# The last queries' scores as two products over equal halves of the keys

## The chip, the cores and the metric

The kernel runs on one core of one Trainium2 chip. The metric is the device time of one execution in microseconds (us); of several runs the median is given. Matrix products run on TensorE (PE in the profile, its weight loads PEld), most elementwise work on VectorE (DVE), exponentials and casts on ScalarE (ACT), some scaling and subtracting on GpSimd (POOL), and nearly all transfers are issued from one queue, that of SyncE (SP).

## The reference

Block-causal attention feeds two feed-forward layers, all in float32:

```python
scores = scale * np.matmul(q, k.transpose(0, 1, 3, 2))   # q, k, v: (4, 8, 576, 64)
mask = block_i >= block_j                                # blocks of 64 positions
scores = np.where(mask, scores, -1000000000.0)
scores = scores - np.max(scores, axis=-1, keepdims=True)
attn = np.exp(scores)
attn = attn / (np.sum(attn, axis=-1, keepdims=True) + 1e-09)
attn_out = np.matmul(attn, v)
...
h = x @ w_in;  x = (h * sigmoid(h)) @ w_out              # 2304 tokens, 512 -> 2048 -> 512
h = x @ w_in2; x = (np.maximum(h, 0) + alpha * np.minimum(h, 0)) @ w_out2
```

The last block of 64 queries of each head (positions 512 to 575) sees all 576 keys, so it needs no mask.

## The kernel before

Float32 accuracy is had from three products each: every operand is split into a high and a low part, and high*high, high*low and low*high are summed in PSUM. `product` (L546) yields the three matmuls of a score tile, `three` (L794) those of the feed-forward layers; all feed-forward matmuls carry L797.

Attention is cut into jobs, one for a batch and a pair of heads. Eight `FirstJob`s and eight `Job`s of kind 0 do the first 256 queries; sixteen `Job`s of kind 1 do queries 256 to 511 and the last 64. A job of kind 1 has, in the order of its steps, `scores(2)` (six matmuls with 384 keys, the two heads in the two halves of the array's rows), `scores(3)` (the same with 512 keys), `last_scores` (the change), and their `weights`, which divide by the sum, split in two float16 parts on POOL (L648) and DVE (L650), and turn the tile by a DMA; `output` (L671, products with the values) and `last_output` (L741) come a job or two later. `bound` is one small product (L528), `prepare` casts queries and keys for a later job on ACT (three activations that write `qk`) and DVE (L515, L518).

`last_scores` handles the last 64 queries of both heads at once: 128 query rows by 576 keys. 576 float32 columns are more than one PSUM bank of 512, so the scores take two tiles, `s` and `s2`: 512 keys and 64 keys. The row maximum is the smaller of two negated maxima (L692, L694, L696), then two activations take the exponential with that bias and sum it (`p` from `s`, `pb` from `s2`). All score tiles come in turn from a ring of PSUM tags `"ees"` (two buffers of `e`, one of `s`): `scores(2)` takes an `e` and the `s`, `scores(3)` two of `e`, `last_scores` the `s` and an `e`. So the `scores(2)` of the next job can write `s` only when the exponential has read the `s` of this job's `last_scores`.

The feed-forward work of layer 1 runs between: `up1` (tile `h`, 24 matmuls of 256 columns for a pair of weight tiles) and `down1` (tile `acc`, 24 likewise) alternate, in chunks of 256 tokens; two such pairs go with one job. When a chunk is done `store1` scales its two accumulators into tiles `x2e` (ACT, DVE) and a DMA writes them out; `x2e` shares the two buffers of tag `t` with the tanh tiles of `act1`. Layer 2 follows when attention is over.

The order of all instructions on all engines is made ahead by a list scheduler, `Plan.order` (L131): every step has an engine, a cost (`pe_cost`, `dve_cost`, `act_cost`, ...), what it reads and writes, and a due time `at`; the engine that can start first takes, of the steps that are ready, the one with the smallest due time. A change in a cost can so move steps on every engine:

```python
start = max(free, min(o.ready for o in lst))
...
o = min((o for o in ready[e] if o.ready <= start), key=lambda o: (o.at, o.index))
```

## Time and profile before

| | us |
|---|---|
| median of 3 runs | 988.57 (987.9 to 990.77) |
| the profiled execution | 991.2 |
| its span, first to last instruction | 989.4 |
| PE busy | 965.6 (98% of the span) |
| PEld busy | 889.6 (90%) |
| DVE busy | 634.5 (64%) |
| ACT busy | 392.5 (40%) |
| POOL busy | 255.4 (26%) |

The profile shows one execution. The busy time of PE counts matmuls whose ends are modelled and overlap, so what a matmul costs in a row of them is read from the starts: the start of the next one less its own. The sixteen jobs of kind 1 with their feed-forward work lie between about 211 and 467 us from the start of the span, layer 2 after about 585 us.

### The profile page before, as it was taken

The numbers are of one execution on the slowest core, as the hardware profiler recorded it, in microseconds if no ns is written. First come the engines' busy times: TensorE is split into PE (matmuls) and PEld (weight loads), VectorE is DVE, ScalarE is ACT, GpSimd is POOL, SyncE is SP. The second block draws the span as 40 slices with busy tenths as digits, with TensorE's granted clock in tenths as the row PEclk, the third lists the DMA queues.
The fourth block names the chain that finished last, engine by engine and source line by source line (L and its number), as shares of the span: only waits on it lengthen the run. The fifth ranks groups of instructions, "written<-read, shape, count | busy, mean of one in ns | idle before, by whom it ended". The sixth has DMA issues, their size and how long they took to land.

```text
span 989.4 us, 18146 instructions
## 1 busy us (share of the span) xinstructions
PE 965.6 (98%) x7072; PEld 889.6 (90%) x7072; DVE 634.5 (64%) x1365; ACT 392.5 (40%) x904; POOL 255.4 (26%) x312
## 2 busy tenths in 40 slices
PE   7889999999999999999999999999999999999998
PEld 5789999899999989999999989999999999999997
DVE  5999976668877778787124999844444444444443
ACT  5876744445555555554224555421111211211111
POOL 2632222435444445454223550010100100100000
PEclk9989999999999999999999999999999999999999
DMA  9940333456685765654215970010010100000100
GB/s 367 360 169 23 76 97 102 73 111 129 108 164 111 145 128 132 122 120 89 37 54 204 331 253 1 1 64 1 1 64 1 64 1 1 33 1 1 32 1 32
DMA packets 124469, 94.04 MB, mean 95 GB/s; under 512 B 98400, under 2 KB 109792, under 8 KB 124384
## 3 DMA queue, kind: packets, MB, share of 16 engines
q1 hardware_dynamic: 124384, 92.90, 35.2%
q8 instruction: 55, 0.90, 0.4%
q14 instruction: 30, 0.25, 0.1%
HBM read 60.37 MB, written 9.96 MB: 71 GB/s over the span
## 4 chain that ended last, share of the span: by engine, by line
PE 83%; DVE 10%; DMA 3%; issue 2%; ACT 2%; POOL 0%; SPq 0%; POOLq 0%; DVEq 0%; ACTq 0%
PE h L797 27%; PE acc L797 24%; PE e L797 15%; PE s L797 7%; PE e L550 3%; PE s L550 2%; PE o L671 2%; DMA pT<-p 1%; DMA x<-x2e 1%; DVE ws1i L344 1%; PE o L741 1%; DVE p L650 1%; DVE t L830 1%; PE o L528 1%; DVE g L311 1%
## 5 line engine op out<-in xcount | busy, mean ns | idle before, releaser
L797 PE MATMUL h<-xh,w0i 128*128 128x256 f32 x1728 | 231.9, 288 | 3.4 <-DVE w0i L311 3.2
L797 PEld LDWEIGHTS h<-xh,w0i 128*128 128x128 f32 x1728 | 217.8, 194 | 6.7 <-DVE w0i L311 3.4
L797 PE MATMUL acc<-g,w0o 128*128 128x256 f32 x1536 | 203.3, 286 | 3.8 <-DVE g L311 3.7
L797 PEld LDWEIGHTS acc<-g,w0o 128*128 128x128 f32 x1536 | 190.0, 191 | 6.4 <-DVE g L311 5.4
L301 ACT ACTIVATE g<-u 128x384 fp32r<-128x384 f32 x96 | 50.2, 523 | 267.5 <-DVE u L915 265.9
L797 PE MATMUL e<-w1o,g 128*128 128x512 f32 x576 | 148.8, 394 | 0.0
L797 PEld LDWEIGHTS e<-w1o,g 128*128 128x128 f32 x576 | 106.7, 188 | 16.8
L797 PE MATMUL acc<-xh,w1i 128*128 128x384 f32 x576 | 109.1, 337 | 0.0
L797 PE MATMUL h<-xh,w1i 128*128 128x384 f32 x576 | 108.9, 337 | 0.0
L797 PEld LDWEIGHTS acc<-xh,w1i 128*128 128x128 f32 x576 | 102.4, 188 | 4.2
L797 PEld LDWEIGHTS h<-xh,w1i 128*128 128x128 f32 x576 | 102.3, 188 | 4.0
L830 DVE SCALAR_TENSOR_TENSOR t<-t,h 128x512 f32<-128x512 f32 x72 | 49.0, 681 | 62.5 <-ACT t L301 62.1
L311 DVE TENSOR_TENSOR g<-u,g 128x384 fp32r<-128x384 f32 x96 | 54.4, 567 | 53.8 <-ACT g L301 53.8
L648 POOL TENSOR_SCALAR p<-p,stat 128x384 f16<-128x384 f32 (+3 forms) x96 | 60.3, 635 | 105.0 <-ACT g L301 35.1
L311 POOL TENSOR_TENSOR xh<-xs,xh 128x384 fp32r<-128x384 f32 x20 | 21.0, 1082 | 244.9 <-ACT xh L301 244.9
L311 POOL TENSOR_TENSOR g<-t,g 128x512 fp32r<-128x512 f32 x48 | 66.4, 1384 | 67.7 <-ACT g L301 64.2
L797 PE MATMUL s<-w1o,g 128*128 128x512 f32 x288 | 82.0, 392 | 0.0
L301 ACT ACTIVATE t<-h 128x512 f32<-128x512 f32 x72 | 42.8, 595 | 90.4 <-PE h L797 79.9
L650 DVE SCALAR_TENSOR_TENSOR p<-p,stat,p 128x384 f16<-128x384 f32 (+3 forms) x96 | 68.8, 732 | 11.6 <-POOL p L648 11.5
L913 DVE TENSOR_SCALAR u<-acc,alpha_sb 128x384 f32<-128x384 f32 x48 | 29.6, 617 | 72.0 <-PE acc L797 71.8
L913 DVE TENSOR_SCALAR u<-h,alpha_sb 128x384 f32<-128x384 f32 x48 | 29.6, 616 | 68.6 <-PE h L797 68.6
L797 PEld LDWEIGHTS s<-w1o,g 128*128 128x128 f32 x288 | 54.1, 188 | 12.5
(121 smaller groups left out, 1244.5 us busy)
## 6 DMA issues: line engine op xcount, KB each, us to landing
st<-qkv_b SPq DMA_DIRECT2D x16, 800.0 KB, 5.1
raw0i<-w_in SPq DMA_DIRECT2D x16, 512.0 KB, 10.2
raw0o<-w_out SPq DMA_DIRECT2D x16, 512.0 KB, 10.3
raw1i<-w_in SPq DMA_DIRECT2D x16, 512.0 KB, 5.2
raw1o<-w_out SPq DMA_DIRECT2D x16, 512.0 KB, 4.8
x<-x2e SPq DMA_DIRECT2D x18, 256.0 KB, 4.1
st<-qkv_first SPq DMA_DIRECT2D x8, 512.0 KB, 7.3
st<-qkv_a SPq DMA_DIRECT2D x8, 512.0 KB, 3.6
```

The source lines that it names most:

```text
L301: nc.scalar.activation(dst(), src(), func, **k)
L311: eng.tensor_tensor(lo(), src(), hi().bitcast(F32), op=ALU.subtract)
L344: add("DVE", dve_cost(512), lambda: nc.vector.scalar_tensor_tensor(t(), t(), 3, low(), op0=ALU.logical_shift_left, op1=ALU.bitwise_or), [t ...
L528: add("PE", 0.25, lambda: nc.tensor.matmul(t()[:, 0:128], am()[:, 0:1].to_broadcast([128, 128]), eye_sb(), start=True, stop=True), [am, ey ...
L550: yield lambda n=n, a=a, b=b: nc.tensor.matmul(dst, w[rows, a, q0:q0 + m], w[rows, b, nq + k0:nq + k1], start=(n == 0), stop=(n == 2))
L648: add("POOL", pool_cost(n), lambda hl=hl, rr=rr, pr=pr: nc.gpsimd.tensor_scalar(hl()[:, :, 0], pr(), rr(), 1.0, op0=ALU.mult, op1=ALU.mult ...
L650: add("DVE", dve_cost(n, 1, 1), lambda hl=hl, rr=rr, pr=pr: nc.vector.scalar_tensor_tensor(hl()[:, :, 1], pr(), rr(), hl()[:, :, 0], op0=A ...
L671: nc.tensor.matmul(o()[64 * r:64 * r + 64, q0:T1], self.v(r, kt, cv), self.pT[r][1]()[:, 2 * kt + cp, q0:T1], start=(kt == 0 and n == 0), ...
L741: nc.tensor.matmul(o()[64 * r:64 * r + 64, 0:64], self.v(r, kt, cv), pT()[:, run, 64 * r:64 * r + 64], start=(run == 0 and cv == 0), stop= ...
L797: nc.tensor.matmul(dst, lhs(a), rhs(b), start=(start and n == 0), stop=(stop and n == 2))
L830: add("DVE", dve_cost(2 * T1), lambda: nc.vector.scalar_tensor_tensor(t(), t(), 1.0, h3(), op0=ALU.add, op1=ALU.mult), [t, h], [t])
L913: add("DVE", dve_cost(T2, 1, 1), lambda: nc.vector.tensor_scalar(u(), h()[:, 0:T2], 0.0, alpha_sb()[:, m:m + 1], op0=ALU.min, op1=ALU.mult ...
```

## The change

The 576 keys are cut into 288 and 288 in place of 512 and 64. The cost that the scheduler is given for the products goes from three matmuls of 512 columns and three counted as 100 to six of 288. There are still two maxima, now over 288 columns each. `p` (512 columns) and `pb` (64) keep their shapes, so the exponential takes three activations: 288 columns from `s` and 224 from `s2` into `p`, 64 from `s2` into `pb`, with three sums. The two small DVE steps of `last_weights` before the reciprocal add three sums in place of two and then the 1e-9; their number stays three.

```diff
@@ -684,33 +684,34 @@
             x = sb(att_p, [128, 10], F32, "stat", 4, name="stat4")
             s, s2 = ps_scores(self.k), ps_scores(self.k)
             def products():
-                for dst, a, b in ((s, 0, 512), (s2, 512, 576)):
+                for dst, a, b in ((s, 0, 288), (s2, 288, 576)):
                     for f in self.product(dst()[:, 0:b - a], slice(0, 128), 256, 128, a, b):
                         f()
 
-            add("PE", pe_cost(*[512] * 3, *[100] * 3), products, [qk], [s, s2], after=self.beside(-1, "output"))
-            add("DVE", dve_cost(512), lambda: nc.vector.tensor_reduce(
-                x()[:, 0:1], s(), axis=AX.X, op=ALU.max, negate=True), [s], [(x, 0)])
-            add("DVE", dve_cost(64), lambda: nc.vector.tensor_reduce(
-                x()[:, 1:2], s2()[:, 0:64], axis=AX.X, op=ALU.max, negate=True), [s2], [(x, 0)])
+            add("PE", pe_cost(*[288] * 6), products, [qk], [s, s2], after=self.beside(-1, "output"))
+            for n, half in enumerate((s, s2)):
+                add("DVE", dve_cost(288), lambda n=n, half=half: nc.vector.tensor_reduce(
+                    x()[:, n:n + 1], half()[:, 0:288], axis=AX.X, op=ALU.max, negate=True), [half], [(x, 0)])
             add("DVE", dve_cost(80), lambda: nc.vector.tensor_tensor(
                 x()[:, 2:3], x()[:, 0:1], x()[:, 1:2], op=ALU.min), [(x, 0)], [(x, 1)])
             p = sb(att_p, [128, 512], F32, "p", 3)
             pb = sb(att_p, [128, 64], F32, "p4b", 2)
             bias = lambda: x()[:, 2:3]
-            act(512, lambda: p(), lambda: s(), AF.Exp, [s, (x, 1)], [p, (x, 2)], psum=True,
-                bias=bias, accum_out=lambda: x()[:, 4:5])
-            act(64, lambda: pb(), lambda: s2()[:, 0:64], AF.Exp, [s2, (x, 1)], [pb, (x, 3)], psum=True,
-                bias=bias, accum_out=lambda: x()[:, 5:6])
+            for n, (dst, src, a, b) in enumerate((
+                (lambda: p()[:, 0:288], s, 0, 288), (lambda: p()[:, 288:512], s2, 0, 224), (lambda: pb(), s2, 224, 288),
+            )):
+                act(b - a, dst, lambda src=src, a=a, b=b: src()[:, a:b], AF.Exp, [src, (x, 1)],
+                    [(p, n) if n < 2 else pb, (x, 2 + n)], psum=True, bias=bias, accum_out=lambda n=n: x()[:, 4 + n:5 + n])
             self.xp[4] = x, p, pb
 
         def last_weights(self):
             x, p, pb = self.xp.pop(4)
-            add("DVE", dve_cost(1, 1, 1), lambda: nc.vector.tensor_scalar(
-                x()[:, 6:7], x()[:, 4:5], x()[:, 5:6], EPS, op0=ALU.add, op1=ALU.add), [(x, 2), (x, 3)], [(x, 4)])
+            add("DVE", dve_cost(1, 1, 2), lambda: nc.vector.tensor_scalar(
+                x()[:, 7:8], x()[:, 4:5], x()[:, 5:6], x()[:, 6:7], op0=ALU.add, op1=ALU.add),
+                [(x, 2), (x, 3), (x, 4)], [(x, 5)])
             add("DVE", dve_cost(1), lambda: nc.vector.tensor_scalar(
-                x()[:, 6:7], x()[:, 6:7], 2.0**-P_EXP, None, op0=ALU.mult), [(x, 4)], [(x, 4)])
-            add("DVE", dve_cost(6), lambda: nc.vector.reciprocal(x()[:, 8:9], x()[:, 6:7]), [(x, 4)], [(x, 5)])
+                x()[:, 7:8], x()[:, 7:8], EPS, 2.0**-P_EXP, op0=ALU.add, op1=ALU.mult), [(x, 5)], [(x, 5)])
+            add("DVE", dve_cost(6), lambda: nc.vector.reciprocal(x()[:, 8:9], x()[:, 7:8]), [(x, 5)], [(x, 6)])
             rr = lambda: x()[:, 8:9]
             p16 = self.parts16(0)
             hl = lambda: p16()[:, 0:8].rearrange("p (j c) m -> p j c m", c=2)
@@ -721,10 +722,10 @@
             ):
                 b = pb if key else p
                 add("POOL", pool_cost(n), lambda src=src, hi=hi: nc.gpsimd.tensor_scalar(
-                    hi(), src(), rr(), 1.0, op0=ALU.mult, op1=ALU.mult), [b, (x, 5)], [(p16, key)])
+                    hi(), src(), rr(), 1.0, op0=ALU.mult, op1=ALU.mult), [b, (x, 6)], [(p16, key)])
                 add("DVE", dve_cost(n, 1, 1), lambda src=src, hi=hi, lo=lo: nc.vector.scalar_tensor_tensor(
                     lo(), src(), rr(), hi(), op0=ALU.mult, op1=ALU.subtract),
-                    [b, (x, 5), (p16, key)], [(p16, key + 1)])
+                    [b, (x, 6), (p16, key)], [(p16, key + 1)])
             pT = self.pT4 = sb(att_p, [128, 9, 128], F16, "pT4")
             self.transpose(lambda: pT(), lambda: p16().rearrange("p a m -> p (a m)"), 9, [p16], [pT])
 
```

The numbers of the scheduler's other steps are the same, but their order is not: from the first `last_scores` on it differs on every engine, up to the sixteenth; the instructions ahead of that and the last 471 rows on PE, from the end of attention to the end, stand as before.

On PE, at the `last_scores` of the twelfth of the sixteen jobs, before (`s` and `e` are the score tiles, `acc` and `h` the feed-forward tiles, the last six rows `scores(2)` of the next job, which need that `s`):

```order
L550 MATMUL s<-qk 128x512 x3
L550 MATMUL e<-qk 128x64 x3
L797 MATMUL acc<-g,w0o_1007 128x256 x12
L797 MATMUL acc<-g,w0o_1040 128x256 x12
L797 MATMUL h<-xh_4236,w0i_1264 128x256 x12
L550 MATMUL e<-qk 128x384
L550 MATMUL s<-qk 128x384
L550 MATMUL e<-qk 128x384
L550 MATMUL s<-qk 128x384
L550 MATMUL e<-qk 128x384
L550 MATMUL s<-qk 128x384
```

and in the changed kernel:

```order
L550 MATMUL s<-qk 128x288 x3
L550 MATMUL e<-qk 128x288 x3
L798 MATMUL acc<-g,w0o_1007 128x256 x12
L798 MATMUL acc<-g,w0o_1040 128x256 x12
L550 MATMUL e<-qk 128x384
L550 MATMUL s<-qk 128x384
L550 MATMUL e<-qk 128x384
L550 MATMUL s<-qk 128x384
L550 MATMUL e<-qk 128x384
L550 MATMUL s<-qk 128x384
```

The twelve `h` matmuls that stood between have moved behind `scores(2)`: the next job's products with `s` stand directly behind the 24 `acc` matmuls. It is so in ten of the sixteen jobs; in two (the seventh and the eleventh) three `h` matmuls stay between, in the first three 18, 12 and 6, and the sixteenth has no `scores(2)` behind it.

On PE further on, from the end of the same `last_output` to the next `output`, before (`e` 128x512 x6 is `scores(3)`, `o<-eye_sb,am` is `bound`):

```order
L797 MATMUL h<-xh_4236,w0i_1303 128x256 x12
L797 MATMUL acc<-g,w0o_1178 128x256 x12
L797 MATMUL acc<-g,w0o_1212 128x256 x6
L550 MATMUL e<-qk 128x512 x6
L528 MATMUL o<-eye_sb,am 128x128
L797 MATMUL acc<-g,w0o_1212 128x256 x6
L797 MATMUL h<-xh_4236,w0i_1502 128x256 x12
L797 MATMUL h<-xh_4236,w0i_1573 128x256 x12
```

and in the changed kernel:

```order
L798 MATMUL h<-xh_4243,w0i_1264 128x256 x12
L798 MATMUL h<-xh_4243,w0i_1303 128x256 x12
L550 MATMUL e<-qk 128x512 x6
L528 MATMUL o<-eye_sb,am 128x128
L798 MATMUL acc<-g,w0o_1178 128x256 x12
L798 MATMUL acc<-g,w0o_1212 128x256 x12
L798 MATMUL h<-xh_4243,w0i_1502 128x256 x12
L798 MATMUL h<-xh_4243,w0i_1573 128x256 x12
```

`scores(3)` and `bound` have moved ahead of 18 `acc` matmuls. It is so behind most jobs; behind the sixth, the tenth and the fourteenth they stand after 12 of the 24. A `store1` falls ahead of the `last_scores` of the second, sixth, tenth and fourteenth job, in both orders after 18 of the `acc` matmuls of the rows above; in the changed order `scores(3)` and `bound` of these jobs (but for the second) come ahead of those 18.

On DVE at the `last_scores` of the same job, before (`p_...` are the float16 parts of the weights of `scores(3)`, `xh` an attention output, `qk` the casts of a later job):

```order
L830 SCALAR_TENSOR_TENSOR t<-t,h 128x512
L650 SCALAR_TENSOR_TENSOR p_5867<-p,stat,p_5867 128x4x128
L650 SCALAR_TENSOR_TENSOR p_5870<-p,stat,p_5870 128x4x128
L764 SCALAR_TENSOR_TENSOR xh_5334<-o,sc,xh_5334 128x256
L692 TENSOR_REDUCE stat_5900<-s 128x1
L515 SCALAR_TENSOR_TENSOR qk<-st,qk 128x384
L694 TENSOR_REDUCE stat_5900<-e 128x1
L518 TENSOR_TENSOR qk<-st,qk 128x576
L696 TENSOR_TENSOR stat_5900<-stat_5900 128x1
```

and in the changed kernel:

```order
L650 SCALAR_TENSOR_TENSOR p_5848<-p,stat,p_5848 128x4x128
L831 SCALAR_TENSOR_TENSOR t<-t,h 128x512
L650 SCALAR_TENSOR_TENSOR p_5878<-p,stat,p_5878 128x4x128
L765 SCALAR_TENSOR_TENSOR xh_5345<-o,sc,xh_5345 128x256
L693 TENSOR_REDUCE stat_5905<-s 128x1
L693 TENSOR_REDUCE stat_5905<-e 128x1
L695 TENSOR_TENSOR stat_5905<-stat_5905 128x1
L515 SCALAR_TENSOR_TENSOR qk<-st,qk 128x384
L518 TENSOR_TENSOR qk<-st,qk 128x576
```

The two casts of `qk` stand behind the maximum in place of between its parts; in five jobs (the first three, the seventh and the eleventh) one or both still stand ahead of its last step. On ACT, in the sixth, tenth and fourteenth job, the exponentials stand ahead of the last cast of `qk`, elsewhere behind the three casts as before.

## Rows read from the trace of the kernel before

**Rows 1.** The page, part 1: busy us of each engine (share) and instructions.

```profile
PE 965.6 (98%) x7072; PEld 889.6 (90%) x7072; DVE 634.5 (64%) x1365; ACT 392.5 (40%) x904; POOL 255.4 (26%) x312
```

**Rows 2.** A stretch: its length, busy PE, PEld, DVE, ACT, POOL, granted clock, DMA, GB/s.

```profile
380.00:470.00 90.00, 89.98 (x925) 83.01 (x921) 69.61 (x176) 45.64 (x115) 42.28 (x53) 1.00 0.54 112
```

**Rows 3.** Timeline of PE by start, twelfth job: start us, us, engine, line.

```profile
397.83 0.96 PE L550 MATMUL s<-qk 128*128 128x512 f32 x3
398.63 0.41 PE L550 MATMUL e<-qk 128*128 128x64 f32 x3
398.88 3.11 PE L797 MATMUL acc<-g,w0o 128*128 128x256 f32 x24
401.83 1.60 PE L797 MATMUL h<-xh,w0i 128*128 128x256 f32 x12
403.36 0.44 PE L550 MATMUL e<-qk 64*128 64x384 f32 x1
...
408.42 0.97 PE L550 MATMUL e<-qk 64*128 64x512 f32 x6
...
409.56 0.96 PE L797 MATMUL acc<-g,w0o 128*128 128x256 f32 x6
```

**Rows 4.** Timeline of PE, first job, where feed-forward matmuls stand ahead.

```profile
211.72 0.86 PE L550 MATMUL s<-qk 128*128 128x512 f32 x3
212.41 0.41 PE L550 MATMUL e<-qk 128*128 128x64 f32 x3
```

**Rows 5.** The chain that ended last: runs of 256 and of 384 columns.

```profile
486.29 2.88 PE acc L797 x24
...
594.32 2.10 PE h L797 x12
```

**Rows 6.** DVE by line and form, 210 to 470 us: count, busy us, mean ns.

```profile
L692 DVE TENSOR_REDUCE stat<-s 128x1 f32<-128x512 f32 x16 | 10.8, 678 | 0.0
...
L694 DVE TENSOR_REDUCE stat<-e 128x1 f32<-128x64 f32 x16 | 3.4, 213 | 0.0
```

**Rows 7.** Timeline of DVE and ACT, twelfth job; in brackets idle before, its releaser.

```profile
397.90 1.41 DVE L650 SCALAR_TENSOR_TENSOR p<-p,stat,p 128x512 f16<-128x512 f32 x2
...
399.94 1.10 ACT L301 ACTIVATE qk<-st 128x384 fp32r<-128x384 f32 x2
...
402.02 0.69 ACT L301 ACTIVATE p<-s,stat 128x512 f32<-128x512 f32 x1 [0.98 <-DVE stat L696]
...
402.70 0.30 ACT L301 ACTIVATE p4b<-e,stat 128x64 f32<-128x64 f32 x1
```

**Rows 8.** Timeline behind the third job: `scores(2)` and the exponential it waits for.

```profile
250.69 0.69 ACT L301 ACTIVATE p<-s,stat 128x512 f32<-128x512 f32 x1 [2.40 <-DVE stat L696]
250.96 0.44 PE L550 MATMUL e<-qk 64*128 64x384 f32 x1
...
251.52 0.44 PE L550 MATMUL s<-qk 64*128 64x384 f32 x1
```

**Rows 9.** Timeline behind the second job, the same two products.

```profile
234.15 0.44 PE L550 MATMUL e<-qk 64*128 64x384 f32 x1
...
234.54 0.44 PE L550 MATMUL s<-qk 64*128 64x384 f32 x1
```

**Rows 10.** Timeline about the tenth job, ahead of which a chunk is stored.

```profile
357.19 0.59 ACT L301 ACTIVATE x2e<-acc 128x512 f32<-128x512 f32 x1
...
361.77 1.34 PE L671 MATMUL o<-pT,v 128*64 128x256 f16 x24
...
363.80 0.60 ACT L301 ACTIVATE t<-h 128x512 f32<-128x512 f32 x1 [2.75 <-DMA x<-x2e]
...
368.57 0.44 PE L550 MATMUL e<-qk 64*128 64x384 f32 x1
...
369.81 0.44 PE L550 MATMUL s<-qk 64*128 64x384 f32 x1 [0.79 <-ACT p L301]
```

**Rows 11.** Tile `x2e`, 200 to 470 us: its eight stores.

```profile
DMA to landing us min/median/max: 2.3/4.0/5.9
```

## The prediction

> **What bounds the kernel now.** I read the page's busy shares first: PE is busy for 98% of the span, DVE for 64%, ACT for 40% [rows 1]. A share is an average, so the second view was the windows: in the stretch that holds the later jobs PE is busy for all but 0.02 of 90 us, at the full granted clock (1.00, the 2.4 GHz level), while DVE has 20 us to spare, ACT and POOL more than 44 [rows 2]. So in that stretch the time is the sum of what PE's instructions take from start to start, plus its few waits; work added to DVE, ACT or POOL costs nothing until it makes PE wait. The third view, the timeline of PE, gives those spacings [rows 3 to 5], and the same view about the `scores(2)` of each job gives the waits, which stand in three places alone: 0.56 us behind the third job [rows 8], 0.39 behind the second [rows 9], 1.24 behind the tenth [rows 10], together 2.19. Each is the same wait: the first product into `e` starts, the one into `s` stands until the exponential of the last queries has read `s`.
>
> **The products themselves.** A run of 24 matmuls of 256 columns takes 2.88 us, 0.120 each; twelve of 384 columns take 2.10, 0.175 each [rows 5]. The three of 512 columns take 397.83 to 398.63 = 0.80 us, the three of 64 columns 398.63 to 398.88 = 0.25, and the 24 behind them 398.88 to 401.83 = 2.95 in place of 2.88 [rows 3]. So a product of 64 columns costs (0.25 + 0.07)/3 = 0.107 us, nearly what one of 256 does: under some width the columns no longer set the pace. That is the waste which the change removes. Of the 0.80, 0.11 belongs to the products with the values that stand ahead, since the first job, where a feed-forward run stands ahead, needs only 212.41 - 211.72 = 0.69 [rows 4]; it stays. A matmul of 288 columns isn't in the trace; between 256 and 384 it is 0.120 + 0.055 x 32/128 = 0.134. Its bounds are those two rows, 0.120 and 0.175; I take 0.134, since 512 columns (0.69/3 = 0.230) lie on the same line. Before: 0.80 + 0.25 + 0.07 = 1.12 us a job. After: 6 x 0.134 + 0.11 = 0.91. Saved 0.21 a job, in sixteen jobs (the count in [rows 6]) 3.4 us; with the bounds, 4.7 at best and 0.6 lost at worst.
>
> A rule that speaks against this: the Trainium skill ("TensorE: Matmul & The Clock Gate", Back-to-back issue gap) gives, for pairs of weight load and matmul in a real kernel, 81 ns sustained at 128 columns and 131 at 512. A line through these, an estimate from that page, gives 73 ns at 64 and 102 at 288, so 3 x 131 + 3 x 73 = 612 before and 6 x 102 = 612 after: no gain. The trace differs at the wide end, with 230 ns at 512 columns.
>
> **The other engines.** DVE: maxima over 512 and 64 columns took 0.678 + 0.213 = 0.891 us; on the line between them one over 288 takes 0.213 + 224 x 0.465/448 = 0.445, two 0.891: nothing changes [rows 6]. ACT: exponentials of 512 and 64 columns took 0.69 and 0.30 [rows 7], so 0.87 ns a column; 288, 224 and 64 take 0.49 + 0.44 + 0.30 = 1.23 in place of 0.99. That adds 0.24 us a job, 3.9 in all, beside at least 44 us of idle ACT in 90 [rows 2]; the reading of the sum lies within these (the next activation starts 0.68 after the 0.69 one), so I add nothing for it. Were there no cover it would delay the division by 0.24 a job; the turned weights are wanted two jobs later, so PE doesn't see it. The small DVE steps keep their number; a second sum as an operand may cost some tens of ns, hidden likewise.
>
> **What the new order does.** The shorter products change the scheduler's costs, and `scores(2)` moves from behind twelve `h` matmuls to directly behind the 24 `acc` ones. Its start, counted from the start of `last_scores`, is now 403.36 - 397.83 = 5.53 us [rows 3]; it becomes 5.53 - 12 x 0.120 - 0.21 = 3.88. When is `s` free? Between the start of the exponential and the start of the waiting product lie 251.52 - 250.69 = 0.83 us [rows 8]; with 288 columns in place of 512 it is 0.83 - 0.20 = 0.63. The exponential starts 4.19 us after `last_scores` now, behind DVE, whose maximum is late: the two L650 steps run until 399.31, and the casts stand between the maxima [rows 7]. In the new order `scores(3)` stands 18 matmuls (2.2 us) earlier, so L650 is through before, and the casts follow the maximum. ACT is then the limit: its casts end at 399.94 + 1.10 = 401.04, 3.21 after `last_scores`, and follow the attention output as before. So `s` is free at 3.21 + 0.63 = 3.84 and PE asks at 3.88. That holds in ten jobs, three of them with a store; the margin is 0.04, where it was 5.53 - 4.19 - 0.83 = 0.51. I count 0.05 a job for the other seven, 0.3, with bounds of 0 and 0.3 a job. The first three jobs keep some `h` matmuls; the second asks 0.9 earlier than before but its `scores(3)` is 0.7 earlier too, so 0.3 of wait.
>
> The jobs with a store are the weak spot. `x2e` holds a buffer that the next `t` needs; in the tenth job `t` waited 2.75 us for the DMA, ACT ran late and PE waited 1.24 [rows 10]. `x2e` started 361.77 - 357.19 = 4.58 ahead of the products with the values; in the new order `scores(3)` and `bound` (409.56 - 408.42 = 1.14 [rows 3]) no longer stand between, so 3.4. With the median landing of 4.0 us [rows 11] behind 0.6 of `x2e`, `t` starts 1.2 after those products do. In the tenth job 369.81 - 363.80 = 6.01 us passed from `t` to the product that waited; PE now asks 1.3 + 3.88 = 5.2 after the products with the values begin. At worst only the exponential's 0.20 comes off the 6.01, and PE waits 1.2 + 5.8 - 5.2 = 1.8; at best, with DVE's two casts and ACT's last one now behind the exponential, some 1.5 more comes off (an estimate; ACT's two casts take 1.10 together [rows 7], DVE's two of the same tiles are as long or longer) and PE waits 0.3. With a landing of 2.3 nothing waits, with 5.9 each is 1.9 more. I take 0.5 for each of three jobs, 1.5, near the lower end because the casts are seen to move. Sum of waits after: 0.3 + 0.3 + 1.5 = 2.1, as many as the 2.19 before. From the end of attention the order is the same, and moves as a whole.
>
> **The sum.** Of the profiled 991.2 us (989.4 of span, 1.8 around it): -3.4 from the products, -0.1 from the waits, so 987.7. The median is 988.57, 2.6 below the profiled run; the same step gives 985.1. Since the margins can only be eaten from one side I round towards the waits: 985.4.
>
> **Rivals.**
> A wait in place of the products: the ten `scores(2)` that ask at 3.88 find `s` taken a little longer, or the stores land late. For it: a margin of 0.04, and a wait at just that place three times already. Against it: sixteen jobs lost only 2.19 together. At 0.1 more in each of ten jobs and 1 more over the stores, 2 of the 3.4 are gone: 987.2.
> The columns alone set the pace, so that 1728 columns before and after take the same (this is what the page's line comes to): 988.6. Against it: 0.107 a matmul at 64 columns [rows 3].
> Slower: the casts on ACT or the maxima on DVE end 0.7 late in each of the ten jobs, because GpSimd and VectorE work at other times than now; PE then stands 0.7 ten times, 7.0 - 3.4 = 3.6 lost: 992.2. It decides from 0.34 a job on. Against it: ACT's casts ended at 3.21 with a `t` and a `g` ahead, which the new order leaves there.
> Better: the products as forecast, and no wait anywhere: 988.57 - 3.4 - 2.2 = 983.0.
>
> **How the numbers follow.** Forecast 0.50, the wait 0.31, columns alone 0.08, slower 0.05, better 0.06. A measurement of this kernel can tell about 0.3%, 3.0 us, so the line lies at 985.6, just above the forecast. Faster: 0.47 of the forecast and the better case, 0.53; same: the wait, columns alone and the rest, 0.42; slower 0.05. The range is 983.0 to 988.6.
>
> **What would show it.** Right: the three products into `s` and into `e` at 0.40 us each (0.5 where products with the values stand ahead), the 24 `acc` behind them at 2.88, the same clock, and under 0.3 us between the first product into `e` and the one into `s` in most of the ten jobs. Wrong: products of 288 columns at more than 0.15 us each; or a wait on ACT's `p` at every `scores(2)`; or waits on DVE or DMA at places where PE now has none.

## The result and the profile after

The changed kernel is slower: 998.19 us (median of six runs, 994.95 to 999.16) against 989.18 for the kernel before (six runs beside them, 986.89 to 990.77), a ratio of 1.0089 [1.007, 1.0108]. The forecast was 985.4. A second series gave 997.04 against 990.52, 1.0063 [1.0042, 1.0085].

Part 1 of the page of the changed kernel, and its window of 380 to 470 us (columns as in [rows 1] and [rows 2]):

```profile
PE 964.2 (97%) x7072; PEld 886.6 (89%) x7072; DVE 655.8 (66%) x1365; ACT 397.4 (40%) x936; POOL 253.7 (26%) x312
```

```profile
380.00:470.00 90.00, 88.32 (x880) 80.76 (x879) 75.74 (x174) 45.93 (x122) 39.90 (x53) 1.00 0.56 109
```

PE, which stood for 0.02 of these 90 us before [rows 2], now stands for 1.68, and finishes fewer matmuls in them (880 against 925, though the window also cuts the jobs at other places); DVE is busy for 6 us more, with no instruction added. The clock is the same.

The place where it shows is PE's timeline at the twelfth job, as in [rows 3]:

```profile
399.09 0.66 PE L550 MATMUL s<-qk 128*128 128x288 f32 x3
...
399.59 0.56 PE L550 MATMUL e<-qk 128*128 128x288 f32 x3
...
399.99 3.04 PE L798 MATMUL acc<-g,w0o 128*128 128x256 f32 x24
...
402.95 0.44 PE L550 MATMUL e<-qk 64*128 64x384 f32 x1
...
403.78 0.44 PE L550 MATMUL s<-qk 64*128 64x384 f32 x1 [0.39 <-ACT p L301]
```

The six products take 399.99 - 399.09 = 0.90 us where they took 1.05, and `scores(2)` begins 3.86 after `last_scores`; both are as forecast. But the product into `s` begins 0.83 after the one into `e`: PE waits for the exponential. DVE, ACT and POOL at the same job, to be read beside [rows 7]:

```profile
398.23 1.36 POOL L648 TENSOR_SCALAR p<-p,stat 128x512 f16<-128x512 f32 x2 [1.00 <-DVE stat L637]
398.96 1.17 DVE L650 SCALAR_TENSOR_TENSOR p<-p,stat,p 128x512 f16<-128x512 f32 x1 [0.98 <-POOL p L648]
...
400.06 0.68 DVE L831 SCALAR_TENSOR_TENSOR t<-t,h 128x512 f32<-128x512 f32 x1
400.65 0.74 DVE L650 SCALAR_TENSOR_TENSOR p<-p,stat,p 128x512 f16<-128x512 f32 x1
400.76 0.63 ACT L301 ACTIVATE g<-t 128x512 fp32r<-128x512 f32 x1 [1.09 <-DVE t L831]
...
402.15 1.10 ACT L301 ACTIVATE qk<-st 128x384 fp32r<-128x384 f32 x2
...
403.15 0.48 ACT L301 ACTIVATE p<-s,stat 128x288 f32<-128x288 f32 x1
```

ACT's casts end at 403.25, 4.16 after `last_scores`, where 3.21 was forecast: `g` waits 1.09 us for DVE's `t`, `t` stands on DVE behind the first L650, and that waits 0.98 for POOL.

The jobs are best compared over one stretch, from the start of the first `last_scores` to the start of the sixteenth. Before, that is 464.69 - 211.72 [rows 4] = 252.97 us; after, 467.73 - 208.97 = 258.76; in a second profile of the changed kernel 470.75 - 211.49 = 259.26. Before:

```profile
464.69 0.96 PE L550 MATMUL s<-qk 128*128 128x512 f32 x3
```

and after, in the first profile:

```profile
208.97 0.56 PE L550 MATMUL s<-qk 128*128 128x288 f32 x3
...
467.73 0.66 PE L550 MATMUL s<-qk 128*128 128x288 f32 x3
```

So 5.8 to 6.3 us of the loss lie in these jobs. What lies ahead of and behind the stretch takes 208.6 to 211.8 and 523.6 to 529.1 us in the profiles of all kernels here, with no order that follows the change. TensorE's clock accounts for a part of that: where the granted clock from 140 to 205 us is 0.97 (before, and the second profile of the changed kernel, among others) the stretch begins at 210.9 to 211.8, where it is 1.00 (the first profile of the changed kernel, among others) at 208.6 to 209.9; `scores2_behind_12` stands apart with 211.4. Behind the stretch the four longest, 527.1 to 529.1, have 0.97 or 0.98 in some part of 470 to 600 us, the others 1.00 there. The rest of the medians' difference, up to 3 us, is not shown by the profiles.

### The profile page after: what moved, and what is told of

The parts are those of the page before. It is cut to its first block, busy times and chain, and to the rows that moved or that the text cites. A ratio compares the mean times of both kernels' runs of the same rounds, so it can differ in the third digit from the quotient of the medians.

```text
span 993.2 us, 18217 instructions
## 1 busy us (share of the span) xinstructions
PE 964.2 (97%) x7072; PEld 886.6 (89%) x7072; DVE 655.8 (66%) x1365; ACT 397.4 (40%) x936; POOL 253.7 (26%) x312
## 4 chain that ended last, share of the span: by engine, by line
PE 66%; DVE 17%; issue 6%; ACT 5%; POOL 2%; DMA 2%; POOLq 0%; ACTq 0%; DVEq 0%; SPq 0%
PE h L798 21%; PE acc L798 18%; PE e L798 15%; PE s L798 7%; DVE p L650 3%; ACT p L301 2%; DVE stat L609 2%; DVE t L831 2%; POOL p L648 1%; PE s L550 1%; DVE ws1i L344 1%; ACT qk L301 1%; DVE p L726 1%; PE o L671 1%; PE e L550 1%
## 5 line engine op out<-in xcount | busy, mean ns | idle before, releaser
L798 PE MATMUL h<-xh,w0i 128*128 128x256 f32 x1728 | 227.8, 286 | 4.3 <-DVE w0i L311 3.5
L798 PEld LDWEIGHTS h<-xh,w0i 128*128 128x128 f32 x1728 | 214.8, 192 | 7.8 <-DVE w0i L311 3.9
L798 PE MATMUL acc<-g,w0o 128*128 128x256 f32 x1536 | 200.7, 285 | 3.8 <-DVE g L311 3.8
L650 DVE SCALAR_TENSOR_TENSOR p<-p,stat,p 128x384 f16<-128x384 f32 (+3 forms) x96 | 84.0, 893 | 23.4 <-POOL p L648 23.3
L311 DVE TENSOR_TENSOR g<-u,g 128x384 fp32r<-128x384 f32 x96 | 54.5, 568 | 53.8 <-ACT g L301 53.8
L311 POOL TENSOR_TENSOR g<-t,g 128x512 fp32r<-128x512 f32 x48 | 64.8, 1350 | 82.5 <-ACT g L301 82.3
L311 POOL TENSOR_TENSOR xh<-xs,xh 128x384 fp32r<-128x384 f32 x20 | 21.0, 1077 | 244.7 <-ACT xh L301 244.7
L648 POOL TENSOR_SCALAR p<-p,stat 128x384 f16<-128x384 f32 (+3 forms) x96 | 56.6, 600 | 95.2 <-DVE stat L637 35.1
L301 ACT ACTIVATE p<-e,stat 128x384 f32<-128x384 f32 (+3 forms) x94 | 50.9, 544 | 44.6 <-DVE stat L609 40.3
```

Source lines behind the costliest of these rows:

```text
L301: nc.scalar.activation(dst(), src(), func, **k)
L311: eng.tensor_tensor(lo(), src(), hi().bitcast(F32), op=ALU.subtract)
L648: add("POOL", pool_cost(n), lambda hl=hl, rr=rr, pr=pr: nc.gpsimd.tensor_scalar(hl()[:, :, 0], pr(), rr(), 1.0, op0=ALU.mult, op1=ALU.mult ...
L650: add("DVE", dve_cost(n, 1, 1), lambda hl=hl, rr=rr, pr=pr: nc.vector.scalar_tensor_tensor(hl()[:, :, 1], pr(), rr(), hl()[:, :, 0], op0=A ...
L798: nc.tensor.matmul(dst, lhs(a), rhs(b), start=(start and n == 0), stop=(stop and n == 2))
```

## The experiments

In the table "wait" is the time from the first product of `scores(2)` into `e` to the first into `s`, summed over the fifteen jobs that have one behind them (it is 0 where PE doesn't wait); "job" is the time from one `last_scores` to the next that occurs most often, or its usual range. Both come from the starts in each run's timeline of PE, as does the stretch. (The 2.26 of the kernel before are the prediction's 2.19 and 0.07 in the first job.)

| kernel | us | ratio to before | stretch | wait | job |
|---|---|---|---|---|---|
| before | 989.2 to 991.0 | 1 | 252.97 | 2.26 | 16.77 |
| the change | 998.19 | 1.0089 [1.007, 1.0108] | 258.76 | 11.47 | 17.0 to 17.4 |
| `changed_kernel_again` | 997.04 | 1.0063 [1.0042, 1.0085] | 259.26 | 12.00 | 17.0 to 17.4 |
| `halves_old_order` | 1005.38 | 1.0145 [1.012, 1.017] | 264.63 | 16.68 | 17.76 |
| `old_split_new_order` | 992.44 | 1.0026 [1.0007, 1.0045] | 255.28 | 4.62 | 16.77 |
| `tanh_before_low` | 990.23 | 1.0003 [0.9985, 1.002] | 250.52 | 3.23 | 16.55 |
| `scores2_behind_12` | 1001.42 | 1.0113 [1.0089, 1.0138] | 261.02 | 8.95 | 16.6 to 19.1 |
| `third_exponential` | 1002.91 | 1.0123 [1.01, 1.0145] | 265.12 | 14.17 | 17.77 |
| `halves_two_exponentials` | 997.27 | 1.0072 [1.0051, 1.0093] | 258.42 | 10.83 | 17.34 |
| `short_subtract_before` | 988.24 | 0.9971 [0.9958, 0.9984] | 250.69 | 0.00 | 16.77 |
| `short_subtract_halves` | 985.13 | 0.9946 [0.9928, 0.9964] | 248.85 | 1.58 | 16.55 |
| `short_subtract_after` | 984.82 | 0.9945 [0.9923, 0.9967] | 247.61 | 0.32 | 16.55 |
| `memset_for_subtract` | 986.74 | 0.9955 [0.994, 0.997] | 247.76 | 0.47 | 16.55 |
| `one_late_job` | 993.26 | 1.0023 [1.0006, 1.0039] | 253.93 | 3.22 | 16.77 |
| `maxima_before_low` | 993.69 | 1.0032 [1.0018, 1.0046] | 255.88 | 7.08 | 16.55 |
| `maxima_and_tanh_first` | 991.11 | 1.0007 [0.9988, 1.0025] | 253.51 | 6.22 | 16.55 |
| `tanh_first_early_maxima` | 989.79 | 0.9998 [0.9985, 1.0011] | 251.07 | 3.77 | 16.55 |
| `tanh_first_maxima_in_three` | 988.11 | 0.9982 [0.9969, 0.9995] | 250.06 | 2.77 | 16.55 |
| `subtract_on_vector` | 987.83 | 0.9979 [0.9963, 0.9994] | 249.49 | 2.20 | 16.55 |
| `before_subtract_on_vector` | 990.40 | 1.0006 [0.9991, 1.0021] | 251.79 | 0.52 | 16.0 to 18.1 |

**Was it the new order?** Two kernels take the change apart. In the first the scheduler is told the costs of before, so that the halves run in the order of before:

```diff
-            add("PE", pe_cost(*[288] * 6), products, ...
+            add("PE", pe_cost(*[512] * 3, *[100] * 3), products, ...
-                add("DVE", dve_cost(288), lambda n=n, half=half: ...
+                add("DVE", dve_cost((512, 64)[n]), lambda n=n, half=half: ...
...
+                    planned=(act_cost(512, True, 1, True), 0.0, act_cost(64, True, 1, True))[n])
```

> The two halves of 288 keys, but the scheduler is told the costs of the split 512 and 64 (the second exponential is told as nothing), so every engine's instructions stand in the order of the kernel before, with one activation more a job. Theory (the order is what cost the time, the halves themselves save): the products take 0.21 to 0.23 us less a job and scores(2) waits no more than the 2.2 us in all of before, so 3.4 to 3.7 us less than before, about 985.5 where before is 989, ratio 0.9963. Rival (the halves themselves hold the score tile s longer, by a third activation and a longer second maximum): the waits of 0.4 to 1.4 us behind each job stay, about 11 us in all, and the time is that of the changed kernel, 995 to 999. Second rival (both): near 989.

In the second 512 and 64 keys run in the changed order, by the same means:

```diff
-            add("PE", pe_cost(*[512] * 3, *[100] * 3), products, ...
+            add("PE", pe_cost(*[288] * 6), products, ...
```

> The split 512 and 64 of before, but the scheduler is told the costs of the halves, so every engine's instructions stand in the order of the changed kernel (one activation less a job). Theory (the order): the waits of the changed kernel, 11 us, and 0.2 us more in each of 13 jobs since the exponential of 512 columns holds s longer, and none of the 3.5 us of shorter products: 998 + 3.5 + 2 = 1003, at least 1000. Rival (the halves themselves): the time of before, 989.

Both came out the other way: 1005.38 and 992.44. The order of before doesn't save the halves, it makes them worse; the new order costs the old split 2.5 us. My theory, that the new order alone did it, fell. Moving single steps of the changed order back gave half an answer. First, on DVE, the first L650 of `scores(3)` ("low30") goes behind the tanh step `t` (`dve[i]`):

```diff
+        for o in [o for o in ops if o.what == "low30"]:
...
+            behind(o, dve[i])
```

> The changed kernel with one step moved on DVE alone: in each job the product that makes the tanh tile t (L831 of the changed kernel) stands again ahead of the first low part of the weights of scores(3) (L650), which waits for GpSimd. Theory (DVE's queue: t stands behind an instruction that waits, so g and ACT's casts of qk and the exponential come late): the exponential starts 0.5 to 0.9 us earlier, the wait at scores(2) falls from 0.44 to 0.97 to under 0.3 in most jobs, 6 to 8 us less than the changed kernel: 990 to 992. Rival (DVE is simply full there, its work since scores(3) ends as late whatever the order): under 2 us less, 996 to 998.

It came in as expected (990.23): with `t` ahead of L650 `g` and the casts are early again and a job takes 16.55 us; the waits that stay are in the first three jobs (2.59 of 3.23). And on PE, `scores(2)` (at `i`) put back behind twelve `h` matmuls, four steps of three:

```diff
+            for n in range(ahead, 4):
+                j = next(j for j in range(i, len(ops)) if ops[j].what == "up")
+                ops.insert(i, ops.pop(j))
```

> The changed kernel with one step moved on PE alone: scores(2) stands again behind the first twelve h matmuls, 1.44 us later, where it stood before; all other engines keep the changed order. Theory (scores(2) asks for s before the exponential has read it, and the rest of the order is harmless): in the jobs from the fourth on the waits of 0.44 to 1.27 us are covered, 9 to 10 us less than the changed kernel, 986 to 989. Rival (the chain on DVE and ACT paces the jobs, not PE's place in it): the wait moves to another place and less than half comes back, over 993.

That fell as well (1001.42): PE asks 1.44 us later, the exponential starts 0.94 later too (5.26 us after `last_scores` in place of 4.32, means over fifteen jobs), and a job takes 17.40 in place of 17.25. The mean hides two things. Eleven jobs became shorter together, 16.85 us each in place of 17.27; the first (19.46 in place of 16.21) and the sixth, tenth and fourteenth (19.10, 18.56 and 18.50 in place of 17.40, 17.82 and 17.41) became longer. In these three, which have a store, PE now waits at `scores(3)` as well, for ACT's exponential:

```profile
311.12 0.96 PE L550 MATMUL e<-qk 64*128 64x512 f32 x5 [0.60 <-ACT p L301]
```

And the first job's loss isn't that of the order of before: the edit put the first `scores(2)` behind twelve `h` matmuls too, where it stands in neither kernel; PE then waited 2.10 us, and the 18 `acc` matmuls behind took 3.74 in place of 2.25 at a mean granted clock of 0.54. So moving PE's question covers a part of the wait and doesn't bring the jobs to 16.55; something else sets their pace. `halves_old_order` shows what, as its order is that of before:

```profile
384.65 0.66 PE L550 MATMUL s<-qk 128*128 128x288 f32 x3
...
385.22 2.88 DVE L650 SCALAR_TENSOR_TENSOR p<-p,stat,p 128x512 f16<-128x512 f32 x2 [0.34 <-POOL p L648]
...
385.85 1.71 POOL L311 TENSOR_TENSOR g<-t,g 128x512 fp32r<-128x512 f32 x1
...
390.52 0.50 ACT L301 ACTIVATE p<-s,stat 128x288 f32<-128x288 f32 x1 [2.81 <-DVE stat L695]
...
391.17 0.44 PE L550 MATMUL s<-qk 64*128 64x384 f32 x1 [0.77 <-ACT p L301]
...
398.25 1.29 POOL L311 TENSOR_TENSOR g<-t,g 128x512 fp32r<-128x512 f32 x1
398.32 1.64 DVE L650 SCALAR_TENSOR_TENSOR p<-p,stat,p 128x384 f16<-128x384 f32 x1
```

The two L650 of 512 columns take 2.88 us here and took 1.41 in [rows 7]; one of 384 columns takes 1.64 while POOL's subtraction L311 runs. In the kernel before the same instruction, beside the subtraction and alone:

```profile
392.73 1.29 POOL L311 TENSOR_TENSOR g<-t,g 128x512 fp32r<-128x512 f32 x1
393.45 0.98 DVE L650 SCALAR_TENSOR_TENSOR p<-p,stat,p 128x384 f16<-128x384 f32 x1
395.16 0.60 DVE L650 SCALAR_TENSOR_TENSOR p<-p,stat,p 128x384 f16<-128x384 f32 x1
```

The new theory: exponential of the last queries, division (L709), maxima and exponentials of the next scores, L648, L650, attention output, maximum, next exponential form a ring over ACT, DVE and POOL from job to job. When it is late, L650 meets the subtraction, takes up to 1.0 us longer, and the ring stays late.

**What makes it late.** The kernel before, its 512-key exponential cut in two (only the lines of the activations are shown):

```diff
-            act(512, lambda: p(), lambda: s(), AF.Exp, ...
-            act(64, lambda: pb(), lambda: s2()[:, 0:64], AF.Exp, ...
+            (lambda: p()[:, 0:288], s, 0, 288), (lambda: p()[:, 288:512], s, 288, 512), (lambda: pb(), s2, 0, 64),
```

> The kernel before (512 and 64 keys, its order on every engine) with one thing of the change: the exponential of the 512 keys is cut in two (288 and 224), so that there are three activations and three sums. Theory: ScalarE and VectorE form a ring from job to job (exponential of the last queries, division, maxima and exponentials of the next scores, their low parts L650, the maximum of the next last queries, that exponential); the third activation makes it 0.3 us longer, which takes its slack, the low parts fall on GpSimd's subtraction and take 1.64 us instead of 0.6 to 0.98, and PE waits at scores(2): 995 to 1005 us, against 990 before. Rival: the slowdown comes with the shorter products themselves, which make PE ask earlier; then this kernel stays at 989 to 991.

1002.91: the third activation, with no change to any product, loses 13 us. One job of it:

```profile
385.72 0.96 PE L550 MATMUL s<-qk 128*128 128x512 f32 x3
385.86 2.89 DVE L650 SCALAR_TENSOR_TENSOR p<-p,stat,p 128x512 f16<-128x512 f32 x2
386.91 1.29 POOL L311 TENSOR_TENSOR g<-t,g 128x512 fp32r<-128x512 f32 x1 [0.42 <-ACT g L301]
391.17 0.50 ACT L301 ACTIVATE p<-s,stat 128x288 f32<-128x288 f32 x1 [2.24 <-DVE stat L696]
...
392.24 0.44 PE L550 MATMUL s<-qk 64*128 64x384 f32 x1 [0.56 <-ACT p L301]
...
403.48 0.96 PE L550 MATMUL s<-qk 128*128 128x512 f32 x3
```

From 385.72 to 403.48 is 17.76 us, as in most of its jobs from the fourth on, where the kernel before takes 16.77. Both parts of the exponential read `s` here, so it is also held 0.24 us longer (392.24 - 391.17 = 1.07 where [rows 8] has 0.83); but the larger part is that the exponential starts late, 391.17 - 385.72 = 5.45 behind `last_scores` where [rows 7] has 4.19. And `halves_old_order` without the third activation, which leaves the exponential of the last 64 keys out:

```diff
-                (lambda: p()[:, 0:288], s, 0, 288), (lambda: p()[:, 288:512], s2, 0, 224), (lambda: pb(), s2, 224, 288),
+            ... ((lambda: p()[:, 0:288], s, 0, 288), (lambda: p()[:, 288:512], s2, 0, 224))
```

> The kernel halves_old_order with two activations in place of three: the exponential of the last 64 keys is left out, and the two steps that would read it read 64 columns of the other keys. Products of 288 and 288, order of before. Theory (the third activation takes the ring's slack): 985 to 989, the low parts beside the subtraction back at about 1.0 us or less. Rival (the shorter products): 1002 to 1006 as with three.

997.27: 8 us better, but not free; the late ring takes 17.34 here. So the theory was half right: either of the two changes is enough, a longer ring or products that end 0.22 us earlier. How much slack there was can be read from DVE in the kernel before (eleventh job): the division, and the step that waits for the next job's scores.

```profile
386.49 0.21 DVE L709 TENSOR_SCALAR stat<-stat 128x1 f32<-128x1 f32 x1 [1.20 <-ACT p4b L301]
...
387.45 0.11 DVE L607 MEMSET e<- 64x64 f32 x1 [0.36 <-PE s L550]
```

DVE stands 0.36 us there, 0.49 in half of the jobs behind the third and 0.19 to 0.58 in all of them but the tenth: so much may this step come later before the next job's maxima do. The third activation takes 0.24 of it and the third sum 0.06, the products 0.22. That alone isn't more than there is. What tips it is which of two instructions starts first, the second L650 of `scores(3)` or the subtraction. The second and third job are late in the kernel before already (waits of 0.40 and 0.56 us; 0.83 and 1.00 with the third activation); at the fourth the two kernels part. Before:

```profile
263.49 0.74 DVE L650 SCALAR_TENSOR_TENSOR p<-p,stat,p 128x512 f16<-128x512 f32 x1
263.59 1.81 POOL L311 TENSOR_TENSOR g<-t,g 128x512 fp32r<-128x512 f32 x1 [0.56 <-ACT g L301]
```

and with the third activation:

```profile
262.00 1.30 POOL L311 TENSOR_TENSOR g<-t,g 128x512 fp32r<-128x512 f32 x1 [0.39 <-ACT g L301]
262.07 1.78 DVE L650 SCALAR_TENSOR_TENSOR p<-p,stat,p 128x512 f16<-128x512 f32 x1
```

Before, L650 starts 0.10 us ahead, takes 0.74, and the subtraction pays; with the third activation it starts 0.07 behind and pays 1.04 itself. From the fourth job to the fifteenth it leads by 0.10 to 0.45 in every job of the kernel before; with the third activation it is 0.04 to 0.08 behind in ten of these twelve and takes 1.78 to 1.80, and in `halves_two_exponentials` 0.02 to 0.04 behind in nine, at 1.80 to 1.83. So some hundredths decide over 1 us of the ring, and a ring that is 1 us longer brings the next L650 late again. This is read from the rows; no run moves that start alone. Whether a single delay is enough was tried in the kernel before, with the 512-key maximum taken four times in one job:

```diff
+            times = 4 if len(late) == 6 else 1
+                x()[:, 0:1], s(), axis=AX.X, op=ALU.max, negate=True) for _ in range(times)], ...
```

> The kernel before; in the sixth of the sixteen jobs alone the maximum over 512 keys is taken four times, so that VectorE is 2.0 us late once. Theory, strong form (the late state keeps itself up also with 512 and 64 keys, since a ring with low parts beside the subtraction takes 17.3 us and PE's work 16.77): the jobs behind it stay late, 0.5 us each, 993 to 998. Rival (before comes back by its own slack, and only the third activation or the shorter products keep the state up): one wait of 1 to 2 us, gone after one or two jobs, 991 to 992.

That job waits 1.69 us, the next one nothing. Its 993.26 lies at the lower edge of the strong form's range, but the jobs behind it take 16.77 again: that form fell. The kernel before comes back from a late job: in the next one its second L650 still starts 0.12 us ahead of the subtraction. The kernels in which it starts behind don't come back.

**Is it the subtraction?** POOL's L311 was cut to 32 of 256 columns, in the kernel before and with the halves in both orders (these kernels leave the low part of the hidden activations out; the line that gives the products the high part in its place is not shown):

```diff
-            eng.tensor_tensor(lo(), src(), hi().bitcast(F32), op=ALU.subtract)
+            eng.tensor_tensor(cut(lo()), cut(src()), cut(hi().bitcast(F32)), op=ALU.subtract)
...
+              (lambda x: x) if n < 2 or n == NB - 1 else (lambda x: x[:, :, 0:32]))
```

> The kernel before with GpSimd's subtraction in layer 1 cut to 32 of 256 columns; the low part of the hidden activations is left out, and the products that would take it take the high part, so PE's work is the same. It is the control for the next: by the theory before has slack on the ring, so 985 to 990, a gain of no more than its few waits. Rival, that the subtraction has no part in it: 989 to 991 here too; the next run decides.

> halves_old_order with the same cut of GpSimd's subtraction. Theory: the low parts L650 are slow because they stand while the subtraction runs; without it they take 0.6 to 0.93 us, the ring is shorter than PE's work again, and the gain of the products appears: 983 to 988, 15 us or more under halves_old_order (1005). Rival, that the third activation alone makes the ring longer by some tenths in each job and the lock only goes with it: 998 to 1003.

> The changed kernel, its own order, with GpSimd's subtraction in layer 1 cut to 32 of 256 columns (the low part of the hidden activations is left out, PE's work is the same). Theory (the low parts L650 that stand beside the subtraction make the ring longer than PE's work): they take 0.6 to 0.95 us, the waits at scores(2) go from 11.5 us to under 3, 984 to 988, that is 10 us or more less than the changed kernel and 1 to 4 less than the kernel before with the same cut (988.24). Rival (the changed order itself, the tanh step behind L650, makes PE wait): 994 to 998.

All three came in as the theory said. With the halves in the old order:

```profile
391.74 0.66 PE L550 MATMUL s<-qk 128*128 128x288 f32 x3
391.81 1.41 DVE L650 SCALAR_TENSOR_TENSOR p<-p,stat,p 128x512 f16<-128x512 f32 x2
392.94 0.47 POOL L311 TENSOR_TENSOR g<-t,g 128x64 fp32r<-128x64 f32 x1 [1.30 <-ACT g L301]
396.02 0.50 ACT L301 ACTIVATE p<-s,stat 128x288 f32<-128x288 f32 x1 [1.21 <-DVE stat L695]
...
397.05 0.44 PE L550 MATMUL e<-qk 64*128 64x384 f32 x1
...
397.05 0.44 PE L550 MATMUL s<-qk 64*128 64x384 f32 x1
```

L650 is back at 1.41 for two, the exponential starts 4.28 after `last_scores` in place of 5.87, and PE's two products start together. The job takes 16.55 us, 0.22 under the 16.77 of the same cut before: that is what the products are worth, and it is what was forecast (0.21). To tell the subtraction's reads from its length and from PE's wait for what it writes, two memsets took its place:

```diff
+                for _ in range(2):
+                    eng.memset(lo().bitcast(F32), 0.0)
```

> halves_old_order with GpSimd's subtraction in layer 1 replaced by two memsets of the same 512 columns (the low part of the hidden activations is left out, zeros stand for it): GpSimd still works there and the products still wait for what it writes, but its instruction reads nothing from SBUF. Theory (the low parts L650, which read two operands from SBUF, stand still while GpSimd's subtraction reads there): L650 beside the memsets keeps its 0.6 us or the 0.9 us it has beside the other GpSimd steps, 984 to 988. Rival (in short_subtract_halves it was not the reads but the shorter GpSimd queue, or the wait of the products for the low part that went with it): 995 to 1005.

```profile
388.84 1.11 POOL L313 MEMSET g<- 128x512 f32 x2
389.14 0.61 DVE L654 SCALAR_TENSOR_TENSOR p<-p,stat,p 128x384 f16<-128x384 f32 x1
```

The low part (here L654) runs wholly beside 1.11 us of POOL work and takes its 0.61; 986.74 in sum. The memsets start earlier than the subtraction did, since they wait for no input, so length and place aren't held exactly; but busy POOL as such costs L650 nothing. The Trainium skill ("SBUF — State Buffer", Who interferes with whom) says so: a DVE instruction with two inputs from SBUF contends with a GpSimd instruction that reads SBUF, not with one that only writes it. The rows agree, 1.64 against 0.61 us. The same section calls the ports that the two share an exclusive lock; in `halves_old_order` L650 ended 0.42 us after the subtraction (399.96 and 399.54), though it takes 0.60 alone, so not quite all of it waited.

**Can the gain be had?** The second move on DVE, the maxima of `scores(3)` ahead of the L650 of `scores(2)` as before, alone and with `t` first ("low2" are the L650 of `scores(2)`, `dve[i]` the maximum):

```diff
+            for o in [o for o in ops if o.what == f"low2{r}"]:
...
+                    behind(o, dve[i])
```

> The changed kernel with one move on VectorE alone: the maxima of scores(3) stand ahead of the low parts of scores(2), as they did before. Theory: the exponentials of scores(3) start about 1 us earlier, the second low part of 384 columns leaves the subtraction (1.64 to about 0.6 to 1.0), and the waits fall: 988 to 993. Rival (the tanh step behind L650 alone decides): 996 to 999.

> The changed kernel with both moves on VectorE alone: the tanh step ahead of the first low part of scores(3), the maxima of scores(3) ahead of the low parts of scores(2). Theory: no waits at scores(2) behind the third job, 985 to 989, the gain of the products at last. Rival (the tanh step was all of it): 990, as with it alone.

993.69 was a little above the range, 991.11 a miss: ordinary jobs take 16.55 in both, but the jobs with a store wait 2.13, 1.05 and 1.00 in the one and 2.00, 1.82 and 0.96 in the other. A long wait can cost more than itself: in the one, the granted clock fell to 0.50 (the 1.2 GHz level) behind the wait of 2.13, and the 24 `h` matmuls there took 4.47 us where the other kernel, at 1.00 behind its wait of 2.00, needs 2.98. From that stretch:

```profile
303.00:304.50 1.50, 1.50 (x9) 1.50 (x8) 1.41 (x2) 0.00 (x0) 1.50 (x3) 0.50 0.10 22
```

So the move was kept for the first jobs alone, in two and then in three of them (`...[:2]`, `...[:3]` in the loop above):

> tanh_before_low with the maxima of scores(3) ahead of the low parts of scores(2) in the first two jobs alone, where maxima_and_tanh_first showed a wait of 0 in place of 1.38 us behind the third job. Theory: 1.2 us less than tanh_before_low (990.2), that is 988 to 990, the same as the kernel before or a little under it; the store jobs keep their small waits. Rival: the shift moves the stores too, and their waits of 1 to 2 us come back: 990 to 992.

> tanh_first_early_maxima with the move of the maxima in three jobs in place of two, so that it stands ahead of the third job's scores as well, whose wait of 1.39 us stayed. Theory: that wait goes, 988 to 989. Rival (another wait in its place): 990.

In two it did not reach the wait of 1.39 us, so that 989.79 lies in the theory's range without its reason; in three it did, and the kernel takes 988.11, a ratio of 0.9982 [0.9969, 0.9995]. The other way is to take the subtraction off POOL:

```diff
-              "DVE" if n < 2 or n == NB - 1 else "POOL")
+              "DVE")
```

> The changed kernel with all of layer 1's subtractions on VectorE, where they were on GpSimd; nothing is left out, the scheduler makes its order anew. Theory: nothing locks the low parts then, 1.0 us and more a low part is won, 0.7 us for each of two subtractions a job is paid; VectorE is about as busy as in the changed kernel, the waits of PE fall to some tenths a job: 984 to 992. Rival (VectorE is then the bound, or the new order puts another wait at scores(2)): 994 to 1005.

> The kernel before with the same move as subtract_on_vector: all of layer 1's subtractions on VectorE, products of 512 and 64 keys, order made anew. It tells how much of that kernel's 987.83 belongs to the halves. Theory: nothing is locked in either, so the difference is that of the products, 0.22 us in each of fifteen jobs: 990 to 992, 3 above. Rival (the gain over before is VectorE's in place of GpSimd's subtraction): 986 to 988, no difference.

With the halves this gives 987.83, 0.9979 [0.9963, 0.9994]; it and the kernel at 988.11 are the only two that leave nothing out and whose interval lies below 1, by some 0.2%. Its L650 and its subtraction follow each other on DVE:

```profile
391.85 1.50 DVE L650 SCALAR_TENSOR_TENSOR p<-p,stat,p 128x512 f16<-128x512 f32 x2
...
394.03 0.68 DVE L311 TENSOR_TENSOR g<-t,g 128x512 fp32r<-128x512 f32 x1
```

The same move without the halves gives 990.40, 2.6 us more (2.3 in the stretch); of the forecast's 3.4 us of products the most is there; the halves wait 2.20 us in sum, all in the three jobs with a store behind the third, the other 0.52. The scheduler made both orders anew, so these differences are those of move and order together. The changed kernel once more:

> The changed kernel once more, for a second profile: the first (994.95) was the fastest of its six runs, the others lie at 998.0 to 999.2. Theory: the rest is more of the same wait; a profile of 998 shows the waits at scores(2) 3 us longer in sum (14 to 15 us in fifteen jobs in place of 11.5), low parts beside the subtraction again at 1.64. Rival: the 3 us lie outside these jobs (in the stores, or in the second layer), and the waits are 11.5 as before.

The second profile (999.78 us, span 998.0) has waits of 12.00 us, not 14 to 15: the rival was right, what the two profiles differ by lies outside these jobs, at least in part where the granted clock is 0.97 in the second and 1.00 in the first (140 to 205 and 540 to 600 us).

## Why the prediction was wrong

**The products** were right: 0.90 us for the six where 0.91 was forecast, and 0.22 us a job wherever nothing waits (16.55 against 16.77). The line through 256, 384 and 512 columns held for 288; that the columns alone set the pace was wrong. (The best bound of the sum is 4.6 us, not 4.7.)

**The other engines** is the step that failed first. The sizes were right: the three exponentials add 0.24 us a job, the division with a second sum 0.06 (273 to 280 ns against 214). But "beside at least 44 us of idle ACT in 90" I added nothing, and "PE doesn't see it" because the turned weights are wanted two jobs later. The division is not only for those weights: it stands on DVE ahead of the next job's maxima. The cover was not ACT's idle time but the 0.19 to 0.58 us in which DVE stood ahead of L607 and, behind it, the 0.10 to 0.45 by which L650 started ahead of the subtraction. `third_exponential` measured the term that I had set to 0: 13 us.

**The new order.** "ACT is then the limit: its casts end ... 3.21 after" failed by 0.95 us in the twelfth job. I held that a `t` and a `g` stay ahead as before; but in the order of DVE shown above `t` has moved behind the first L650, which waits for POOL, and ACT's `g` follows `t`. I read the move of the casts in those rows and not that of `t`. With `t` put back the step holds: in `tanh_before_low` PE asks at 3.86 to 4.22 behind the third job and waits for nothing in nine of fifteen jobs. "L650 is through before" failed too: the last L650 of `scores(3)` ends 2.30 us behind `last_scores` in the twelfth job, where it was 1.48. In the changed order one L650 of `scores(2)` starts 0.07 to 0.30 behind the subtraction in each job from the third on and takes 1.63 to 1.65, here the second of the two:

```profile
392.56 2.50 DVE L650 SCALAR_TENSOR_TENSOR p<-p,stat,p 128x384 f16<-128x384 f32 x2 [0.19 <-POOL p L648]
393.12 1.53 POOL L311 TENSOR_TENSOR g<-t,g 128x512 fp32r<-128x512 f32 x1
```

By form on DVE, 210 to 470 us, after (count, busy, mean ns):

```profile
L650 DVE SCALAR_TENSOR_TENSOR p<-p,stat,p 128x384 f16<-128x384 f32 x30 | 36.2, 1234 | 0.5 <-POOL p L648 0.4
L650 DVE SCALAR_TENSOR_TENSOR p<-p,stat,p 128x512 f16<-128x512 f32 x32 | 31.5, 995 | 13.3 <-POOL p L648 13.3
```

and before:

```profile
L650 DVE SCALAR_TENSOR_TENSOR p<-p,stat,p 128x512 f16<-128x512 f32 x32 | 26.6, 865 | 1.3 <-POOL p L648 1.3
L650 DVE SCALAR_TENSOR_TENSOR p<-p,stat,p 128x384 f16<-128x384 f32 x30 | 25.8, 861 | 0.0
```

I took DVE's durations as fixed. A mean of 861 ns over instructions of one form, some of which take 600, says that they aren't.

**The waits** were the term that decides: 2.1 forecast, 11.47 measured. The jobs with a store wait 0.86, 1.27 and 0.86 (0.5 forecast, 0.3 to 1.8 as bounds); the other jobs behind the third 0.44 to 0.97 each, where 0.05 was taken; the first three 0.34, 0.88 and 1.38, where 0.3 in sum was taken.

**The rivals.** "Slower" named the place and nearly the size of a job's wait: casts that end 0.7 late in each of ten jobs because POOL and DVE work at other times, 992.2. That is one of the two mechanisms; that the halves lose still more in the order of before (1005.38) was in no rival, and its time was short by 6 us. I gave it 0.05 on the ground that "the new order leaves there" what stood ahead, and that was the misreading. The range's upper end of 988.6 left it out.

## What to carry to other kernels

An engine at 64% may still carry a ring of waits that is only some tenths shorter than the bound engine's work: before a step on it is costed at nothing, look in its queue for the next wait behind that step, and take at most the idle time there as the cover. Shortening the bound engine's work uses up the same slack as lengthening the ring. And where an instruction's duration depends on what another engine does beside it, a ring that falls late can become longer by falling late: compare the shortest and the mean duration of one form before trusting the sum, and read by how much the one starts ahead of the other.

## What was not expected of the hardware

VectorE's L650 with two inputs from SBUF takes 0.60 us alone (384 columns), 0.90 to 1.65 beside GpSimd's subtraction, 0.61 beside memsets on GpSimd. Which of the two starts first decides who pays: of 512 columns L650 takes 0.74 where it starts 0.10 to 0.45 us ahead, and the subtraction then 1.44 to 1.81; where L650 starts 0.02 to 0.08 behind, it takes 1.78 to 1.83, and the subtraction 1.29 to 1.31. The tanh step (L830 before), which reads one of its inputs from PSUM, keeps its time in all of these kernels (674 to 685 ns as the mean). And moving that subtraction from GpSimd (1.29 us) to the busier VectorE (0.68 us), with the order made anew, made the kernel with the halves 10 us faster.
